# The passage from attention to the experts: where the last value sum, the selections, the token counts, the fourth weight split and the row scaling stand

## The chip, the cores and the metric

The kernel runs on one core of a Trainium2 chip. The core has five engines with a queue of instructions each: TensorE (PE, with its weight loads shown apart as PEld), VectorE (DVE), ScalarE (ACT), GpSimd (POOL) and SyncE (SP, which here only issues DMAs). Each engine starts its instructions in the order of its queue; an instruction that waits holds what is behind it. The metric is device microseconds (us) of one execution; the median of the runs shown counts.

## The reference

```python
q_bits = (einsum('bhsd,dk->bhsk', q, proj) > 0); k_bits = ...      # 6 bits: a bucket for each row
scores = where(q_bucket == k_bucket, q @ k.T / sqrt(64), -1e9)      # 2 x 8 heads, 768 rows, 64 wide
x = softmax(scores) @ v                                             # 1536 tokens x 512
e_idx = argmax(x @ w_gate)                                          # one expert of 8 for each token
out[mask_e] = gate_w * eom * (relu(x[mask_e] @ w1[e]) @ w2[e])      # 512 -> 1024 -> 512
y = elu(out @ w_in) @ w_out                                         # 512 -> 2048 -> 512
```

All of it is float32. The kernel splits each operand into a rounded high part and the remainder (hi and lo, `wh` and `wl`, `xh` and `xl`), and adds three products for one.

## The kernel before

There are three stages one after the other: attention (to about 257 us of the profiled span), the eight experts (267 to 443 us), and the wide layer (to the end). The order of the instructions on each engine is that of the program text, which is written by hand; nothing reorders it.

**End of attention.** `stage_V` (L405) multiplies the probabilities by the values for one half head `m` into a PSUM bank of the pool `ps_o`, which has one bank. `stage_O` (L424) copies it out to `osb` on ACT. The last `m` is `NM - 1`. `stage_R` (L471) turns `osb` into token rows. The pool `ps_s` (two double banks) held the scores, which are done by then.

**The last two groups of tokens.** Tokens come in four groups of 384 (`NG - 2` and `NG - 1` are the last ones), each of three columns `c` of 128. `gate` (L525) returns three lists for a group: `main` finds the expert and the row `rown`, and converts it to the index `idx` (the last two items, `main[15:]`); `after` counts the tokens of each expert into `cnt`; the third list, `scs` for the last group, scatters the 384 token rows to `xs_d` in HBM, with one indirect DMA by POOL for a column, at the place that `idx` names.

**The operand of expert 0.** It is not loaded from HBM. `part_sel` (L860) makes a matrix `sel` of zeros and ones that selects the tokens of a column, `part_head` (L864, ACT) and `part_rest` (L868, DVE) make the scaled rows `xhi` and `xlo`, and `part_move` (L874, PE) multiplies rows by `sel` into the accumulators `xacc`. In `first_xT` (L899) these products run in a fixed order, column by column; then ACT copies the two halves of `xacc` to `hi` (the tile `xt`), DVE takes the remainder `lo`, `totals` (L1045) multiplies `cnt` by ones on PE into `pso` and makes the tables `tab` and `offd` on DVE, and `keep_warm` (L621) issues products that nobody reads.

**Experts.** The weights of an expert come in eight pieces of 512 KB: four of `w1`, four of `w2`. `load_piece` (L98) loads a piece on SP, `split_piece` (L813) splits it (`wh` on ACT, `wl` on DVE) and then lets SP load more; a load waits until the split has freed one of the buffers `wraw`. The splits of pieces 1 to 3 stand ahead of expert 0 (`AHEAD = 4`; piece 0 is split earlier); piece 4 is split behind the second of the eight column blocks `f` of expert 0, piece 5 behind the fourth, piece 6 behind the sixth, piece 7 behind the eighth. `moe_L1` (L1111) takes twelve matmuls for a block into one of three banks `hps`, then ACT (`h`, L1124) and DVE (L1125) empty the bank. `moe_L2` (L1127) takes the eight blocks of `h` in turn into `yps`, four times for an expert. `load_xs` (L1090, SP) loads the rows of an expert from `xs_d`; for expert 1 it stands between the loads of pieces 5 and 6 and waits for the last scatter. `scale_xs` (L837) multiplies its two halves of 128 rows by the gate weight in place; `make_xT` (L1095) transposes them on PE, the first time behind the first `moe_L2` of the expert before.

Of the kernel before, what the change touches and what calls it, by code (L numbers as in the profile page):

```python
# [8 lines left out]
F32 = mybir.dt.float32  # L9
# [3 lines left out]
AF = mybir.ActivationFunctionType  # L13
# [12 lines left out]
def kernel(  # L26
# [15 lines left out]
    nc = tc.nc  # L42
    B, H, S, D = q.shape
    E, DM, F = w1.shape
# [5 lines left out]
    HC = HALF * 128  # L50
# [6 lines left out]
    CAP = 224  # L57
# [3 lines left out]
    NG = 2 * B  # L61
# [53 lines left out]
    ps_s = att.enter_context(tc.tile_pool(name="ps_s", bufs=2, space=PSUM))  # L115
    ps_t = att.enter_context(tc.tile_pool(name="ps_t", bufs=3, space=PSUM))
    ps_o = att.enter_context(tc.tile_pool(name="ps_o", bufs=1, space=PSUM))
# [285 lines left out]
    ops = {}  # L403

    def stage_V(m, part):  # L405
        hd = part_of(m)[0]
        hi, lo = ptt[m]
        if part == 0:
            ops[m] = ps_o.tile([128, HC], F32, tag="o", name="o")
        for kt in (2 * part, 2 * part + 1):  # L410
            for x, t in enumerate((hi, lo)):
                nc.tensor.matmul(  # L412
                    ops[m], vst[hd][:, kt, :], t[:, kt, :], start=(kt == 0 and x == 0), stop=(kt == NC - 1 and x == 1)
                )
# [201 lines left out]
    def both(fs):  # L616
        for f in fs:
            f()

    load_pair(1, "q")  # L620
    def keep_warm(n, end=False):  # L621
        ps = (ps_t if end else ps_o).tile([128, HC], F32, tag="t" if end else "o", name="warm")
        for i in range(n):
            nc.tensor.matmul(ps, ones_b, ones_b[:, None, :].to_broadcast([128, HALF, 128]), start=(i == 0), stop=(i == n - 1))
# [52 lines left out]
    NM = 2 * NH  # L677
# [101 lines left out]
    for pc in range(E * NP):  # L779
        stream.append((pc,))  # L780
        j, i = divmod(pc - W2P, 7)
# [23 lines left out]
    def narrow_ops(n):  # L805
        for _ in range(min(n, len(todo_w2))):
            todo_w2.pop(0)()
        load_ahead()

    AHEAD = 4  # L810
    wsp = {}

    def split_piece(pc, eng=nc.vector, eng_hi=nc.scalar, rest=None):  # L813
        if pc not in wraw:
            return
        r = wraw.pop(pc)
        p, a, n = (m2a, "v", 3) if 0 <= pc < 3 else (m1, "w", 5)
        hi = p.tile([128, PW], F32R, tag=a + "h", name="wh", bufs=n)
        lo = p.tile([128, PW], F32R, tag=a + "l", name="wl", bufs=n)
        if eng_hi is nc.scalar:  # L820
            eng_hi.activation(hi, r, AF.Copy)  # L821
        else:
            eng_hi.tensor_copy(hi, r)
        fs = [lambda: eng.tensor_tensor(lo, r, hi, ALU.subtract)]  # L824
        if rest is None:
            both(fs)
        else:
            rest.extend(fs)
        wsp[pc] = (hi, lo)
        assert stream[taken[0]] == (pc,)  # L830
        taken[0] += 1
        load_ahead()
# [4 lines left out]
    def scale_xs(e, engs):  # L837
        t = xsl[e]
        for a, eng in enumerate(engs):
            x, g = t[:, a, 0:DM], t[:, a, DM:DM + 1]  # L840
            if eng is None:
                continue
            if eng is nc.scalar:
                eng.activation(x, x, AF.Copy, scale=g)
            else:
                eng.tensor_scalar(x, x, g, None, ALU.mult)
# [13 lines left out]
    def part_sel(gi, c, eng=nc.vector):  # L860
        row0, sel = parts[gi][:2]
        eng.tensor_scalar(sel[:, c], ranks, row0[:, c:c + 1], None, ALU.is_equal)
# [5 lines left out]
    def part_rest(gi, c):  # L868
        _, _, xh, xl = parts[gi]
        xg = xw[divmod(gi, 2)]  # L870
        x, g = xg[:, c, 0:DM], xg[:, c, DM:DM + 1]
        nc.vector.scalar_tensor_tensor(xl[:, c], x, g, xh[:, c], ALU.mult, ALU.subtract)

    def part_move(gi, ps, which, dcs=range(KD), stop=None):  # L874
        sel = parts[gi][1]
        for c, i in which:
            y = parts[gi][2 + i]
            for dc in dcs:
                nc.tensor.matmul(
                    ps[dc], y[:, c, dc * 128:(dc + 1) * 128], sel[:, c],  # L880
                    start=((gi, c, i) == (NG - 2, 0, 0)), stop=((c, i) == stop),
                )
# [16 lines left out]
    def first_xT(acc, ps):  # L899
        xT[0] = [t.rearrange("p (c n) -> p c n", c=KD) for t in xt0]  # L900
        hi, lo = xT[0]
        part_move(NG - 2, ps, [(0, 1)])
        first_older(ps, 1)
        part_move(NG - 2, ps, [(1, 1)])
        part_move(NG - 1, ps, [(0, 0), (1, 0)])
        part_move(NG - 2, ps, [(2, 1)])
        part_move(NG - 1, ps, [(2, 0), (0, 1)])
        for i in range(2):
            part_move(NG - 1, ps, [(1, 1), (2, 1)], (2 * i, 2 * i + 1), (2, 1))
        for i in range(2):  # L910
            cs = slice(2 * i, 2 * i + 2)
            nc.scalar.activation(hi[:, cs], acc[i][:, :, 0:CAP], AF.Copy)
            nc.vector.tensor_tensor(lo[:, cs], acc[i][:, :, 0:CAP], hi[:, cs], ALU.subtract)
        totals()
        keep_warm(4, True)

    gates = {}

# [108 lines left out]
    first_older(old[1], 0)  # L1027
    keep_warm(3)
    part_rows(NG - 1)
    for c in (1, 2):  # L1030
        part_sel(NG - 1, c, nc.gpsimd)
    for c in range(HALF):
        part_head(NG - 1, c)
    part_rest(NG - 2, 1)
    part_sel(NG - 1, 0)
    both(main[15:])
    for gi, c in ((NG - 2, 2), (NG - 1, 0), (NG - 1, 1), (NG - 1, 2)):
        part_rest(gi, c)
    both(after)

    cno = gate_p.tile([128, 2, E], F32, name="cno")
    tab = gate_p.tile([1, 3 * E], I32, name="tab")
# [2 lines left out]
    def totals():  # L1045
        pso = ps_o.tile([128, 2, E], F32, tag="o", name="pso")
        nc.tensor.matmul(pso, ones_b, cnt[:, NG], start=True, stop=True)
        nc.vector.tensor_copy(cno, pso)
        nc.vector.tensor_copy(tab[:, 0:2 * E], cno[0:1].rearrange("p a e -> p (a e)"))
        nc.vector.tensor_reduce(tab[:, 2 * E:2 * E + 1], cno[0:1, 0], AX.X, ALU.max)  # L1050
        nc.vector.tensor_tensor(offd, cno[:, 1], ebase, ALU.subtract)
# [59 lines left out]
    def moe_L1(e, f, pc):  # L1111
        if f == 0:
            hT[e] = m1.tile([128, 2, FB1, CAP], F32R, tag="h", name="h")
        hi, lo = xT[e]
        wh, wl = (t.rearrange("p (c f) -> p c f", c=KD) for t in wsp[pc])
        fs = slice(f % 2 * 128, f % 2 * 128 + 128)
        ps = ps_h.tile([128, CAP], F32, tag="h", name="hps")
        terms = [(dc, w, x) for dc in range(KD) for w, x in ((wh, hi), (wh, lo), (wl, hi))]
        if (e, f) == (0, 0):
            terms = [(dc, w, x) for x in (hi, lo) for dc in range(KD) for w in ((wh, wl) if x is hi else (wh,))]  # L1120
        for i, (dc, w, x) in enumerate(terms):
            nc.tensor.matmul(ps, w[:, dc, fs], x[:, dc], start=(i == 0), stop=(i == len(terms) - 1))  # L1122
        h, l = hT[e][:, 0, f], hT[e][:, 1, f]
        nc.scalar.activation(h, ps, AF.Relu)  # L1124
        nc.vector.scalar_tensor_tensor(l, ps, 0.0, h, ALU.max, ALU.subtract)  # L1125
# [28 lines left out]
        nc.gpsimd.memset(x2h.bitcast(F32), 0.0)  # L1154
        nc.gpsimd.memset(x2l.bitcast(F32), 0.0)

    for i in range(1, AHEAD):
        split_piece(i)
        if i == 1:
            load_xs(1)  # L1160
    for e in range(E):
        if e == 0:
            off = 0
        else:
            off = nc.values_load(
                tab[0:1, E + e:E + e + 1], engines=[ENG.Activation, ENG.DVE], min_val=0, max_val=NT,
                skip_runtime_bounds_check_because="a count of some of the tokens",
            )
        for f in range(FB1):
            pc = e * NP + f // 2  # L1170
            moe_L1(e, f, pc)
            narrow_ops(1)
            if f == 1 and e + 1 < E:
                scale_xs(e + 1, (nc.gpsimd, nc.gpsimd))
            if f == 4 and e >= E - NG:
                tids(e - E + NG)
            if f % 2:
                wsp.pop(pc)
                split_piece(pc + AHEAD)
                if e == E - 1 and f == 7:  # L1180
                    split_w2(0)
                take_w2()
        if e == 0:
            first[0] = False
            load_ahead()
        for dc in range(KD):
            pc = e * NP + 4 + dc
            parts = moe_L2(e, dc, pc, off)
            if e == E - 1:
                parts()  # L1190
            narrow_ops(1)
            wsp.pop(pc)
            split_piece(pc + AHEAD)
            if e < E - 1:
                parts()
            if e + 1 < E and dc < 2:
                make_xT(e + 1, dc)
            if e == E - 1 and dc == 0:
                split_w2(1)
            take_w2()  # L1200
            if dc == 2 and e + 2 < E:
                load_xs(e + 2)
# [15 lines left out]
    acc = {}  # L1218
# [203 lines left out]
```

## Time and profile before

| | |
|---|---|
| median of 3 runs | 715.23 us (715.20 to 715.67) |
| profiled execution | 717.73 us, span of the trace 716.0 us |
| PE busy | 701.2 us (98% of the span), 4217 matmuls |
| DVE, ACT, POOL busy | 553.4 (77%), 428.8 (60%), 206.9 us (29%) |
| chain that ended last | PE 49%, issue 33%, DMA 7%, DVE 4%, ACT 3%, POOL 2% |
| mean granted TensorE clock | 0.998 of full speed |

PE is nearly always busy, so time is to be won or lost where PE waits. All that the change touches lies between 252 and 418 us. In the rows further down each line of a timeline is: start in us from the start of the span, duration in us, engine, line, operation, out<-in, shapes, count, and in brackets how long the engine had been idle before and what ended that.

### The profile page before, as it was taken

What the parts mean: (1) busy time and instruction counts of PE and PEld (TensorE: products, weight loads), DVE (VectorE), ACT (ScalarE), POOL (GpSimd) and SP (SyncE); (2) the same over time, 40 slices, a digit from 0 to 9 for tenths busy, and PEclk for the clock granted to TensorE, in tenths of its full rate; (3) what the DMA queues carried; (4) which work ended last, traced back from release to release, by engine and by line L of the source; (5) the groups of instructions that cost most, each with busy time, mean ns of one, the idle gap of its engine ahead of it and who ended that gap; (6) DMA issues with size and microseconds to landing.
All of it is one profiled execution on the core that took longest, in us unless ns stands there. A gap on an engine that the chain in (4) does not pass through costs nothing.

```text
span 716.0 us, 12241 instructions
## 1 busy us (share of the span) xinstructions
PE 701.2 (98%) x4217; PEld 627.7 (88%) x4218; DVE 553.4 (77%) x1043; ACT 428.8 (60%) x857; POOL 206.9 (29%) x507
## 2 busy tenths in 40 slices
PE   8999999999999999999999999999999999999996
PEld 6889999999998989999999989788888888888884
DVE  6979899899998887888888877977788546934433
ACT  5988898888888866666666665444443224422221
POOL 7655544555446471111144131000000000002012
PEclk9999999999999999999999999999999999999999
DMA  7856759577682319988788876222223000001011
GB/s 173 206 130 157 190 139 219 139 176 181 156 228 70 107 72 285 266 255 249 227 240 268 215 214 165 89 89 88 64 92 109 3 0 1 0 1 60 0 60 62
DMA packets 108565, 97.40 MB, mean 136 GB/s; under 512 B 33448, under 2 KB 94696, under 8 KB 108496
## 3 DMA queue, kind: packets, MB, share of 16 engines
q1 hardware_dynamic: 106032, 90.15, 46.8%
q0 software_dynamic: 2304, 6.40, 2.4%
q8 instruction: 35, 0.57, 0.3%
q14 instruction: 34, 0.28, 0.1%
q10 hardware_dynamic: 160, 0.00, 0.0%
HBM read 64.15 MB, written 10.72 MB: 105 GB/s over the span
## 4 chain that ended last, share of the span: by engine, by line
PE 49%; issue 33%; DMA 7%; DVE 4%; ACT 3%; POOL 2%; SPq 0%; POOLq 0%; ACTq 0%; DVEq 0%
PE hps L1122 10%; PE s L349 8%; PE o L412 7%; PE yps L1135 7%; PE t L396 7%; DMA out_dram<-part,tidt 5%; PE yps L1137 3%; PE sp L488 2%; ACT p L376 2%; PE zps L278 1%; PE prep L212 1%; DMA xs<-xs_d 1%; DVE nm L367 1%; PE xTp L1104 1%; DVE ptlo L399 1%
## 5 line engine op out<-in xcount | busy, mean ns | idle before, releaser
L399 DVE TENSOR_TENSOR ptlo<-t,pthi 128x384 fp32r<-128x384 f32 x192 | 99.9, 548 | 16.4 <-ACT pthi L398 14.7
L376 ACT ACTIVATE p<-s,bi,sc 128x768 f32<-128x768 f32 x96 | 96.1, 1001 | 19.7 <-POOL bi L369 18.0
L824 DVE TENSOR_TENSOR wl<-wraw,wh 128x1024 fp32r<-128x1024 f32 x63 | 77.1, 1226 | 22.2 <-ACT wh L821 20.6
L367 DVE TENSOR_REDUCE nm<-s 128x1 f32<-128x768 f32 x96 | 90.9, 947 | 0.3 <-PE s L349 0.3
L398 ACT ACTIVATE pthi<-t 128x384 fp32r<-128x384 f32 x192 | 84.7, 497 | 9.6 <-PE t L396 8.3
L1274 POOL DMA_INDIRECT out_dram<-part,tidt x12 | 11.5, 960 | 263.5 <-DVE part L1271 262.2
L1236 ACT ACTIVATE ee<-gps 128x512 f32<-128x512 f32 x48 | 28.7, 599 | 97.9 <-PE gps L1226 97.9
L1135 PE MATMUL yps<-h,wh 128*128 128x448 f32 x256 | 84.4, 380 | 0.0
L396 PE MATMUL t<-ident,p 128*128 128x128 f32 x576 | 79.6, 273 | 0.0
L1226 PE MATMUL gps<-x2h,vl 128*128 128x512 f32 x192 | 75.9, 395 | 0.0
L349 PE MATMUL s<-ka,qa 128*128 128x384 f32 x192 | 73.5, 384 | 2.2 <-ACT p L376 1.6
L1256 PE MATMUL a<-vh,gh 128*128 128x512 f32 x192 | 75.6, 394 | 0.0
L1256 PE MATMUL a<-vh,gl 128*128 128x512 f32 x192 | 75.4, 393 | 0.0
L1226 PE MATMUL gps<-x2h,vh 128*128 128x512 f32 x192 | 75.3, 392 | 0.0
L1226 PE MATMUL gps<-x2l,vh 128*128 128x512 f32 x192 | 75.2, 392 | 0.0
L1256 PE MATMUL a<-vl,gh 128*128 128x512 f32 x192 | 74.9, 390 | 0.0
L1239 ACT ACTIVATE gh<-ee 128x512 fp32r<-128x512 f32 x48 | 30.4, 633 | 69.2 <-DVE ee L1238 69.2
L1237 DVE TENSOR_SCALAR ee<-ee 128x512 f32<-128x512 f32 x48 | 20.4, 425 | 66.3 <-ACT ee L1236 66.2
L396 PEld LDWEIGHTS t<-ident,p 128*128 128x128 f32 x576 | 67.4, 140 | 4.1 <-DVE ptlo L399 0.5
L412 PE MATMUL o<-pthi,vst 128*128 128x384 f32 x192 | 67.1, 349 | 0.8 <-ACT osb L433 0.6
L821 ACT ACTIVATE wh<-wraw 128x1024 fp32r<-128x1024 f32 x63 | 66.1, 1052 | 0.9 <-DMA wraw<-in_moe_w_dram 0.9
L349 PE MATMUL s<-kb,qb 102*128 102x384 f32 x192 | 65.1, 340 | 0.2
(226 smaller groups left out, 1767.9 us busy)
## 6 DMA issues: line engine op xcount, KB each, us to landing
wraw<-in_moe_w_dram SPq DMA_DIRECT2D x64, 512.0 KB
w<-in_moe_w_in_dram SPq DMA_DIRECT2D x16, 512.0 KB
w<-in_moe_w_out_dram SPq DMA_DIRECT2D x16, 512.0 KB
ka<-khi SPq DMA_DIRECT2D x30, 192.0 KB
xs_d<-zt SPq DMA_DIRECT2D x8, 528.0 KB
xs<-xs_d SPq DMA_DIRECT2D x8, 528.0 KB
raw_k<-in_k_dram SPq DMA_DIRECT2D x16, 192.0 KB
raw_v<-in_v_dram SPq DMA_DIRECT2D x8, 384.0 KB
```

What stands on the lines that cost most here:

```text
L349: nc.tensor.matmul(ps[:, j, 0:HC], opnd[st, "q" + x][0:n1, cb], opnd[st, "k" + x][0:n1, j * HC:(j + 1) * HC], start=(x == "a"), stop=(x == ...
L367: nc.vector.tensor_reduce(nm, sps[n][:, :, 0:HC], AX.XY, ALU.max, negate=True)
L376: nc.scalar.activation(p.rearrange("p (a b) -> p a b", a=2), sps.pop(n)[:, :, 0:HC], AF.Exp, bias=bi, scale=sc, accum_out=sums[hd][:, c:c ...
L396: nc.tensor.transpose(ps[:, a, :], p[:, kt * 128:(kt + 1) * 128], ident)
L398: nc.scalar.activation(ho, ps, AF.Copy)
L399: nc.vector.tensor_tensor(lo[:, HALF * g:HALF * (g + 1), i * 128:(i + 1) * 128], ps, ho, ALU.subtract)
L412: nc.tensor.matmul(ops[m], vst[hd][:, kt, :], t[:, kt, :], start=(kt == 0 and x == 0), stop=(kt == NC - 1 and x == 1))
L824: fs = [lambda: eng.tensor_tensor(lo, r, hi, ALU.subtract)]
L1122: nc.tensor.matmul(ps, w[:, dc, fs], x[:, dc], start=(i == 0), stop=(i == len(terms) - 1))
L1135: nc.tensor.matmul(ps, wh[:, f], h[:, :, f], start=(f == 0), stop=last)
L1226: nc.tensor.matmul(ps, w[:, dc], x[:, dc, th * TC:(th + 1) * TC], start=(dc == 0 and i == 0), stop=(dc == KD - 1 and i == 2),)
L1256: nc.tensor.matmul(ps, x[:, cs], w, start=(fb in first_fb and i == 0), stop=(fb in last_fb and i == 2))
```

## The change

It has five parts.

1. The last value sum (`m == NM - 1`) goes to a bank of `ps_s` instead of the one bank of `ps_o`.
2. Of the last group's three selections two are made on DVE (columns 0 and 1, ahead of the `xlo` of the last two columns of group `NG - 2`) and one on POOL (column 2); before, POOL made columns 1 and 2.
3. In `first_xT` the second half of `hi` is copied by DVE instead of ACT; `main[15:]` (row and index) and `after` (the counts) stand behind the two `lo` on DVE, and `totals` behind them; two warming products instead of four, ahead of `totals`.
4. The split of piece 3 stands behind the first column block of expert 0.
5. For experts 1 to 7 POOL scales the first half of the rows only; ACT scales the second, behind the eighth column block of the expert before.

```diff
@@ stage_V
-            ops[m] = ps_o.tile([128, HC], F32, tag="o", name="o")
+            pool, tag = (ps_s, "s") if m == NM - 1 else (ps_o, "o")
+            ops[m] = pool.tile([128, HC], F32, tag=tag, name="o")
@@ first_xT
+        nc.scalar.activation(hi[:, 0:2], acc[0][:, :, 0:CAP], AF.Copy)
+        nc.vector.tensor_copy(hi[:, 2:4], acc[1][:, :, 0:CAP])
+        keep_warm(2, True)
         for i in range(2):
             cs = slice(2 * i, 2 * i + 2)
-            nc.scalar.activation(hi[:, cs], acc[i][:, :, 0:CAP], AF.Copy)
             nc.vector.tensor_tensor(lo[:, cs], acc[i][:, :, 0:CAP], hi[:, cs], ALU.subtract)
+        both(main[15:])
+        both(after)
         totals()
-        keep_warm(4, True)
@@ ahead of first_xT
     part_rows(NG - 1)
-    for c in (1, 2):
-        part_sel(NG - 1, c, nc.gpsimd)
+    part_sel(NG - 1, 2, nc.gpsimd)
     for c in range(HALF):
         part_head(NG - 1, c)
-    part_rest(NG - 2, 1)
-    part_sel(NG - 1, 0)
-    both(main[15:])
-    for gi, c in ((NG - 2, 2), (NG - 1, 0), (NG - 1, 1), (NG - 1, 2)):
+    for c in range(2):
+        part_sel(NG - 1, c)
+    for gi, c in ((NG - 2, 1), (NG - 2, 2), (NG - 1, 0), (NG - 1, 1), (NG - 1, 2)):
         part_rest(gi, c)
-    both(after)
@@ experts
-    for i in range(1, AHEAD):
+    for i in range(1, AHEAD - 1):
         split_piece(i)
         if i == 1:
             load_xs(1)
...
             moe_L1(e, f, pc)
+            if (e, f) == (0, 0):
+                split_piece(AHEAD - 1)
             narrow_ops(1)
             if f == 1 and e + 1 < E:
-                scale_xs(e + 1, (nc.gpsimd, nc.gpsimd))
+                scale_xs(e + 1, (nc.gpsimd, None))
+            if f == 7 and e + 1 < E:
+                scale_xs(e + 1, (None, nc.scalar))
```

How the order moves on PE, from the last products of `xacc` to the first of expert 0 (`pso` is the product of the counts, `warm` a warming product). Before, the rows from there on (three more pairs like the last follow, and then `hps`):

```order
L879 MATMUL xacc<-sel,xlo 128x224 x12
L1047 LDWEIGHTS ones_b
L1047 MATMUL pso<-cnt,ones_b 128x16
L624 LDWEIGHTS ones_b
L624 MATMUL warm<-ones_b 128x384
```

With the change:

```order
L880 MATMUL xacc<-sel,xlo 128x224 x12
L625 LDWEIGHTS ones_b
L625 MATMUL warm<-ones_b 128x384
L625 LDWEIGHTS ones_b
L625 MATMUL warm<-ones_b 128x384
L1048 LDWEIGHTS ones_b
L1048 MATMUL pso<-cnt,ones_b 128x16
L1123 MATMUL hps<-xt_4296,wh 128x224
```

The product of the counts, which was ahead of four warming products, is now the last instruction ahead of expert 0's first (`hps`), and it still reads `cnt`.

On DVE, from the row of the last group's first column (`row_4458`, what the selections compare with) to the remainder `xt`. Before:

```order
L852 SCALAR_TENSOR_TENSOR row_4458<-g_rk,ohs 128x3
L872 SCALAR_TENSOR_TENSOR xlo<-xw,xhi 128x512
L862 TENSOR_SCALAR sel<-ranks,row_4458 128x224
L587 TENSOR_REDUCE rown<-g_rk 128x3
L588 CAST g_idx<-rown 128x3
L872 SCALAR_TENSOR_TENSOR xlo<-xw,xhi 128x512
L872 SCALAR_TENSOR_TENSOR xlo<-xlast,xhi 128x512 x3
L561 TENSOR_REDUCE cnt<-ohs 128x8
L592 TENSOR_TENSOR g_lt<-g_fm,w_73 128x24
L565 TENSOR_REDUCE cnt<-g_lt 128x8
L569 TENSOR_TENSOR cnt<-cnt 128x16
L913 TENSOR_TENSOR xt_4297<-xacc,xt_4296 128x448 x2
```

With the change:

```order
L863 TENSOR_SCALAR sel<-ranks,row_4458 128x224 x2
L873 SCALAR_TENSOR_TENSOR xlo<-xw,xhi 128x512 x2
L873 SCALAR_TENSOR_TENSOR xlo<-xlast,xhi 128x512 x3
L912 CAST xt_4296<-xacc 128x448
L916 TENSOR_TENSOR xt_4297<-xacc,xt_4296 128x448 x2
L588 TENSOR_REDUCE rown<-g_rk 128x3
L589 CAST g_idx<-rown 128x3
L562 TENSOR_REDUCE cnt<-ohs 128x8
L593 TENSOR_TENSOR g_lt<-g_fm,w_73 128x24
L566 TENSOR_REDUCE cnt<-g_lt 128x8
L570 TENSOR_TENSOR cnt<-cnt 128x16
```

The index `g_idx` and the counts `cnt` moved from ahead of the remainder of `xacc` to behind it, and a second selection came in ahead of the first `xlo`. The order of SP's loads is the same before and after: piece 5, the rows of expert 1, piece 6, piece 7.

## Rows read from the trace of the kernel before

**Rows 1.** Who PE waited for, 266 to 446 us: us, times, longest.
```profile
PE xTp L1104 <- POOL xs L846: 1.4, 1, 1.4
PE hps L1122 <- DVE h L1125: 0.9, 1, 0.9
```

**Rows 2.** Timeline: the last value sum, and ACT between it and its copy.
```profile
253.42 0.44 PE L412 MATMUL o<-pthi,vst 128*128 128x384 f32 x1 [0.58 <-ACT osb L433]
...
255.38 0.71 ACT L844 ACTIVATE xs<-xs 128x512 f32<-128x512 f32 x1
...
256.00 0.47 ACT L433 ACTIVATE osb<-o 128x384 f32<-128x384 f32 x1
```

**Rows 3.** Timeline of DVE, 261 to 268 us.
```profile
261.69 0.52 DVE L862 TENSOR_SCALAR sel<-ranks,row 128x224 fp32r<-128x224 bf16 x1
262.14 0.16 DVE L587 TENSOR_REDUCE rown<-g_rk 128x3 f32<-128x24 f32 x1
...
262.41 0.74 DVE L872 SCALAR_TENSOR_TENSOR xlo<-xw,xhi 128x512 fp32r<-128x512 f32 x1
...
265.18 0.17 DVE L561 TENSOR_REDUCE cnt<-ohs 128x8 bf16<-128x24 bf16 x1
...
265.68 0.17 DVE L569 TENSOR_TENSOR cnt<-cnt 128x16 bf16<-128x16 bf16 x1
266.77 1.16 DVE L913 TENSOR_TENSOR xt<-xacc,xt 128x448 fp32r<-128x448 f32 x2 [0.92 <-ACT xt L912]
```

**Rows 4.** Timeline of PE, 264 to 272.6 us.
```profile
264.50 0.70 PE L879 MATMUL xacc<-sel,xhi 128*128 128x224 f32 x4 [0.57 <-POOL sel L862]
...
266.39 0.18 PE L1047 MATMUL pso<-cnt,ones_b 128*128 128x16 bf16 x1
...
266.94 0.40 PE L1122 MATMUL hps<-xt,wh 128*128 128x224 f32 x1
...
272.11 0.48 PE L1122 MATMUL hps<-xt,wh 128*128 128x224 f32 x2 [0.86 <-DVE h L1125]
```

**Rows 5.** Timeline of POOL: selections, first and last of three scatters, first scaling.
```profile
261.48 2.97 POOL L862 TENSOR_SCALAR sel<-ranks,row 128x224 fp32r<-128x224 bf16 x2
264.62 1.56 POOL L598 DMA_INDIRECT xs_d<-xlast,g_idx  x1 [0.17 <-issue]
...
267.76 0.96 POOL L598 DMA_INDIRECT xs_d<-xlast,g_idx  x1 [0.23 <-issue]
...
276.03 3.27 POOL L846 TENSOR_SCALAR xs<-xs 128x512 f32<-128x512 f32 x2 [7.23 <-DMA xs<-xs_d]
```

**Rows 6.** Timeline of SP's queue: rows of expert 1, then pieces 6 and 7.
```profile
270.64 0.37 SPq L1092 DMA_DIRECT2D xs<-xs_d  x1
271.13 1.45 SPq L107 DMA_DIRECT2D wraw<-in_moe_w_dram  x2
```

**Rows 7.** Timeline: split of piece 6, second layer's first and sixth block, blocks 7 and 8.
```profile
277.70 1.06 ACT L821 ACTIVATE wh<-wraw 128x1024 fp32r<-128x1024 f32 x1 [0.92 <-DMA wraw<-in_moe_w_dram]
...
278.90 0.38 PE L1135 MATMUL yps<-h,wh 128*128 128x448 f32 x1
...
279.94 0.68 DVE L1125 SCALAR_TENSOR_TENSOR h<-hps,h 128x224 fp32r<-128x224 f32 x2
...
280.49 0.38 PE L1135 MATMUL yps<-h,wh 128*128 128x448 f32 x1
```

**Rows 8.** Timeline around the first transposes for expert 7.
```profile
409.39 4.53 POOL L846 TENSOR_SCALAR xs<-xs 128x512 f32<-128x512 f32 x2 [15.22 <-DMA xs<-xs_d]
...
412.61 0.36 ACT L1140 ACTIVATE sum<-yps 128x224 f32<-128x224 f32 x1 [1.29 <-PE yps L1135]
...
413.98 0.55 PE L1104 MATMUL xTp<-ident,xs 128*128 128x128 f32 x3 [1.36 <-POOL xs L846]
```

**Rows 9.** The opening products; busy time, PEclk, DMA share, GB/s of a stretch.
```profile
1.16 4.98 PE L624 MATMUL warm<-ones_b 128*128 128x384 bf16 x15 [1.16 <-DVE eb_b L81]
...
268.00:272.00 4.00, 3.25 (x30) 3.06 (x28) 3.97 (x9) 3.65 (x7) 0.81 (x2) 1.00 0.65 227
```

## The prediction

> **What bounds it now.** I looked first at the shares: PE works nearly all the time, so only PE's waits matter. Then I read who PE waited for from the first expert to the wide layer. There are two waits in 180 us: 1.4 us for POOL's scaled rows and 0.9 us for DVE emptying a bank [rows 1]. Then I read the timelines of the passage, where PE waits for the copy of a value sum [rows 2] and for a POOL selection [rows 4]. Last I read what stands just behind each, because the change moves work onto DVE and ACT and past POOL's and SP's queues. All the waits that the change can remove come to 0.58 + 0.57 + 0.86 + 1.36 = 3.4 us, 0.5% of the run. A difference under 0.2%, or 1.43 us, is about what a measurement of this kernel cannot tell from none.
>
> **Part 1, the last value sum.** PE waited 0.58 us for the one bank [rows 2]. With a bank of its own the sum starts that much earlier. But its copy `osb` starts at 256.00, behind a row scaling on ACT that runs from 255.38 [rows 2] and depends on DVE, not on this sum. So the copy stays where it is, and only the products that do not read it move up: six of the twelve that follow then stand ahead of the copy's end, 256.47, and six behind it as before. I take 0.2 us; the bounds are 0 and 0.58.
>
> **Part 2, the selections.** PE waited 0.57 us for the last of two POOL selections, 1.5 us each [rows 4, 5]. One POOL selection then ends near 263.0 and its wait goes. But two selections on DVE now stand ahead of the `xlo` that the products need next; before, that `xlo` came first and one selection behind it. Selection to next operation is 0.45 us (261.69 to 262.14, [rows 3]), so that `xlo` comes 0.7 to 0.9 us later and PE, which took it at once, waits there instead. From there on 0.57 us of waiting is gone, and some tenths of smaller stops, so the last product of `xacc` comes when it came before. I take nothing; the bounds are 0.3 us either way.
>
> **Part 3, the counts.** Here a wait is added on PE. The count product stands directly ahead of expert 0's first product, and it needs `cnt`, which DVE now makes behind the remainder. DVE's chain, with 0.2 us taken off from part 1: the last product of `xacc` started just ahead of 266.39 [rows 4] and is there 0.2 us later, so DVE's copy of the second half starts at 266.6 - 0.2 = 266.4. It is not in the trace; the two remainders of that size take 0.58 us each [rows 3], and I take 0.5 us. The remainders end near 268.0. Then come row and index, 0.27 us (262.14 to 262.41), and the four counts, 0.67 us (265.18 to 265.85) [rows 3]. `cnt` is ready at 268.9, and the first `hps` starts at 269.0 instead of 266.94 [rows 4].
>
> That is 2.0 us later, but not 2.0 us lost. Before, PE stood 0.86 us ahead of the fourth block, at 272.11, because DVE had three weight splits ahead of the first bank to be emptied [rows 4]. **Part 4** puts the third split behind it. DVE then has two splits left, which it starts when `pso` is through; it empties the first bank near 272.3, and PE, 36 products of 0.118 us on (16 of that width took 264.50 to 266.39, [rows 4]), wants it at 273.2. So that wait goes, and the first layer is 2.06 - 0.86 = 1.2 us late (0.7 to 1.6 over the unknown copy and part 2).
>
> **What else the index holds up.** It also starts the scatters. The first started at 264.62 [rows 5] with POOL free after its selections; now it starts when `idx` is there, at 268.4: 3.8 us later. The load of expert 1's rows waits for the last scatter (it went out 2.9 us after that one started, [rows 5, 6]): it goes out at about 274.4 instead of 270.64. Piece 6 is queued behind it on SP and goes out at 274.9 instead of 271.13.
>
> Piece 6 had no room: ACT already waited 0.92 us for it, until 277.70 [rows 7]. ACT's copies of blocks 7 and 8 stand behind that split, and so do DVE's; block 7 was done at 280.28 (the first of two from 279.94 on), and the second layer, whose sixth block started 1.59 us after its first, at 280.49, wanted it at 280.8 [rows 7]. How fast does piece 6 land now? In 6.57 us, as before: 281.5. It came 7.06 us after the load of the rows, but then piece 5, issued little earlier, was in front (1.67 us lies between the landings of the rows and of piece 6, about the same size, [rows 5, 7]); without that, 279.8; and with each scatter as short as the last (0.96 for 1.56 us, [rows 5]) 279.2. I take the middle, 280.3. Block 7 is then done 2.58 us later, at 282.9, **2.0 us** behind 280.8. This contains the 1.2 us of part 3 and is not added to it: the later of the two counts. Bounds: 1.2 and 3.3 us.
>
> **Part 5, the scaling.** For expert 7 the rows landed at 409.39, POOL took 4.53 us for both halves, and PE stood 1.36 us [rows 8]. POOL's first half alone ends near 411.6. ACT stood idle for 1.29 us before 412.61, behind one split of 1.06 [rows 7, 8], so it is through with the last bank at 410.3 and takes 0.71 us for a half [rows 2]: both are there before PE asks, near 412.6. The wait goes: **-1.36 us** (0 if the rows land over a microsecond later). Seven scalings of 0.71 us come onto ACT; each is followed by a split and then by an idle wait for `yps`, 1.29 us in the case shown [rows 8], and so costs nothing. In the other experts POOL was in time anyway. Two warming products fewer lie inside PE's wait for the counts.
>
> **Sum.** +2.0 - 1.36 = +0.64 us: the profiled execution goes from 717.73 to about 718.4 us. That execution was 2.5 us above the median of the runs; by the median, 715.23 + 0.64 = **715.9 us**.
>
> **The clock, weighed against a rule.** PE will stand idle between the warming products (until 266.5) and 269.0, 2.5 us, longer than any stop in the experts so far. In the stretch with the 0.86 us stop the granted clock is 1.00, the 2.4 GHz level [rows 9]. No row shows a stop of 2.5 us, so I keep full speed. The Trainium skill, "TensorE: Matmul & The Clock Gate", section "Why this matters for your kernels", asks that PE not be left idle for long between bursts of matmuls, or it falls to the half clock; by it the sum could be as in rival B.
>
> **Rivals.**
> - **A, slower: piece 6 lands as late as it is issued.** If the DMA needs its 6.57 us again, expert 0 loses 3.3 us and the sum is +1.9: 717.2 us. It decides from a landing at 281.0 on. For it: the load of the rows took 5.4 us to land. Against: less is in flight.
> - **B, slower: PE falls to 1.2 GHz after the idle stretch.** The opening products, after no work, took 4.98 us [rows 9] for 15 of 384 columns: 0.86 ns a column, against 0.53 for the 224 columns in 0.118 us. If the first layer ran for 5 us at half speed, 2.5 us would be lost, of which the wait for block 7 hides about 1: +0.64 + 1.5 = +2.1, 717.4 us. Against: a stop of 2.5 us is not the start of a program.
> - **C, faster: neither new wait binds.** If the counts are ready sooner, because DVE's small operations overlap, and piece 6 lands by 278, what remains is -1.36 and some 0.3 us of parts 1 and 2: 713.6 us. Against: it needs both, and the order puts `cnt` and `idx` behind three operations of half a microsecond.
> - **D, slower: part 5 doesn't do it.** If the rows of expert 7 land after 410.4, ACT waits in place of POOL and PE still stands: +2.0, 717.2 us. Only expert 7's rows were that late.
>
> **How the numbers follow.** My forecast, 715.9 us with a range of its own of 715.1 to 716.6, has 0.53; A 0.20, B 0.06, C 0.14, D 0.07. Slower by over 0.2% is A, B and D: 0.33. Faster by over 0.2% is most of C: 0.12. Within is 0.55. The range from 713.5 to 717.6 takes in C at its price and leaves out its far half and the far ends of A and B, some 0.2 together.
>
> **What would show it.** The `hps` of expert 0 start near 269 with a wait for the counts ahead of them; no wait for `h` before the fourth block; scatters from 268.4; the load of expert 1's rows near 274.4; ACT waiting for piece 6 until about 280; PE standing some 1 us in the first `yps`; no wait for POOL at expert 7. I am wrong if PE starts `hps` before 268, if block 7 is done by 281, or if a stop stays at expert 7.

## The result, and the profile after

| | before | with the change |
|---|---|---|
| median | 715.3 us (715.20 to 715.67, 4 runs) | 722.0 us (720.12 to 722.58, 4 runs) |
| profiled execution | 717.73 us, span 716.0 | 722.58 us, span 720.9 |
| mean granted TensorE clock | 0.998 | 0.992 |

The ratio is 1.0087 [1.0074, 1.0100]: slower by 6.7 us, above the predicted range. The chain of events was the predicted one: late counts, late index, late scatters, late piece 6, a stop in the first `yps`. Two of its links were longer than I took them, the clock fell twice, and a gain was counted that wasn't there.

Who PE waited for with the change, 266 to 446 us (engine, tile and line waited for: us, times, longest), against [rows 1]:

```profile
PE pso L1048 <- DVE cnt L570: 2.3, 1, 2.3
PE yps L1136 <- DVE h L1126: 1.8, 1, 1.8
```

Both waits of before are gone, POOL's at expert 7 and DVE's ahead of the fourth block, and two larger ones stand in their place. The timeline of PE with the change, against [rows 4, 7]:

```profile
262.76 0.71 PE L880 MATMUL xacc<-sel,xlo 128*128 128x224 f32 x4 [1.10 <-DVE xlo L873]
...
269.25 0.18 PE L1048 MATMUL pso<-cnt,ones_b 128*128 128x16 bf16 x1 [2.31 <-DVE cnt L570]
269.28 0.35 PE L1123 MATMUL hps<-xt,wh 128*128 128x224 f32 x1
...
281.71 0.37 PE L1136 MATMUL yps<-h,wh 128*128 128x448 f32 x1
...
285.59 0.47 PE L1136 MATMUL yps<-h,wh 128*128 128x448 f32 x1 [1.83 <-DVE h L1126]
```

The counts made expert 0 start at 269.28, as forecast (269.0). The timeline of DVE, against [rows 3], shows why:

```profile
261.14 0.91 DVE L863 TENSOR_SCALAR sel<-ranks,row 128x224 fp32r<-128x224 bf16 x2
261.97 1.40 DVE L873 SCALAR_TENSOR_TENSOR xlo<-xw,xhi 128x512 fp32r<-128x512 f32 x2
...
266.63 0.62 DVE L912 CAST xt<-xacc 128x448 fp32r<-128x448 f32 x1 [1.27 <-PE xacc L880]
267.17 1.15 DVE L916 TENSOR_TENSOR xt<-xacc,xt 128x448 fp32r<-128x448 f32 x2
268.23 0.17 DVE L588 TENSOR_REDUCE rown<-g_rk 128x3 f32<-128x24 f32 x1
268.43 0.17 DVE L589 CAST g_idx<-rown 128x3 int32<-128x3 f32 x1
...
269.02 0.17 DVE L570 TENSOR_TENSOR cnt<-cnt 128x16 bf16<-128x16 bf16 x1
```

Copy, two remainders, index and counts stand one behind the other, from 266.63 to 269.19. Now the other branch, that of the index. POOL, against [rows 5] (first and last scatter, first scaling):

```profile
269.38 1.05 POOL L599 DMA_INDIRECT xs_d<-xlast,g_idx  x1 [7.06 <-ACT wh L822]
...
272.26 0.96 POOL L599 DMA_INDIRECT xs_d<-xlast,g_idx  x1 [0.21 <-issue]
...
280.74 1.58 POOL L847 TENSOR_SCALAR xs<-xs 128x512 f32<-128x512 f32 x1 [7.43 <-DMA xs<-xs_d]
```

SP's queue, against [rows 6] (piece 5, the rows of expert 1, piece 6 and what follows):

```profile
271.14 0.37 SPq L107 DMA_DIRECT2D wraw<-in_moe_w_dram  x1
276.75 0.37 SPq L1093 DMA_DIRECT2D xs<-xs_d  x1
277.23 14.93 SPq L107 DMA_DIRECT2D wraw<-in_moe_w_dram  x9
```

What SP's load of these rows waited for, 255 to 300 us, first before, then with the change:

```profile
SPq L1092 <- DMA xs_d<-xlast,g_idx: 0.6, 1, 0.6
SPq L1093 <- DMA xs_d<-xlast,g_idx: 5.1, 1, 5.1
```

ACT at piece 6, against [rows 7]:

```profile
282.92 1.06 ACT L822 ACTIVATE wh<-wraw 128x1024 fp32r<-128x1024 f32 x1 [3.33 <-DMA wraw<-in_moe_w_dram]
```

The load of the rows held SP's queue until 276.75 (forecast 274.4), piece 6 was split from 282.92 (forecast 280.3), and block 7 came for PE at 285.59. Last the stretches, with the busy time of each engine, the granted clock (the column behind POOL), DMA share and GB/s:

```profile
266.00:269.00 3.00, 0.93 (x8) 0.52 (x6) 2.29 (x8) 2.43 (x3) 0.00 (x0) 1.00 0.00 0
269.00:273.00 4.00, 3.75 (x20) 3.76 (x21) 3.30 (x8) 1.03 (x2) 3.19 (x5) 0.58 0.25 89
273.00:286.00 13.00, 11.17 (x94) 10.80 (x93) 7.19 (x11) 7.03 (x13) 1.88 (x3) 1.00 0.90 268
286.00:290.00 4.00, 4.00 (x19) 3.74 (x18) 3.59 (x5) 2.04 (x5) 0.00 (x0) 0.58 1.00 307
290.00:296.00 6.00, 6.00 (x40) 5.67 (x40) 3.41 (x6) 3.60 (x7) 0.00 (x0) 0.99 1.10 285
```

Behind each of the two stops the clock was at 0.58 on the mean of four microseconds: most of that time at the 1.2 GHz level, though PE was working in it. The whole execution shown has a mean granted clock of 0.992, as has one other of the four (722.09 us); the remaining two, which have no profile, show 0.996 (721.92 and 720.12 us), so the clock was low for less time in them.

**One table for all runs.** The start of the selection products wanders by 2 us between executions (255.3 to 257.5), so I count from the first `xacc` product to the first `hps` and first `yps` of expert 0, to the first `hps` of expert 1, and to the first product of the wide layer (`gps`), each read from the PE timeline of the profiled execution. The last column takes in seven more experts, so a few tenths there cannot be put down to one part. Each row is one execution, not always a usual one. Against its run's median, the profiled one was 2.5 us longer in the first row, about 1.3 in e1_warm and 1.2 in e3_index_warm, and 1.4 us shorter in p2_select and b1_best and 1.2 in a1_piece_first.

| run | hps | yps | expert 1 | gps | median us |
|---|---|---|---|---|---|
| before, profile shown | 9.73 | 21.69 | 32.71 | 186.28 | 715.3 |
| p0_before | 9.75 | 21.71 | 32.89 | 184.90 | 715.93 |
| the change | 12.19 | 24.62 | 39.28 | 191.29 | 722.0 |
| e1_warm | 12.21 | 23.01 | 39.41 | 191.44 | 721.82 |
| e2_index | 12.19 | 22.99 | 33.99 | 186.00 | 716.87 |
| e3_index_warm | 13.90 | 24.70 | 35.71 | 187.70 | 717.37 |
| e4_index_counts | 10.00 | 21.55 | 32.85 | 184.87 | 715.35 |
| p1_bank | 9.85 | 21.81 | 32.81 | 184.81 | 715.58 |
| p2_select | 9.82 | 21.78 | 32.79 | 184.80 | 716.4 |
| p4_split | 9.74 | 20.76 | 32.78 | 184.91 | 715.47 |
| p5_scale | 9.75 | 21.71 | 32.88 | 184.97 | 716.1 |
| a1_piece_first | 12.20 | 24.62 | 35.63 | 187.69 | 718.42 |
| a2_piece_first_warm | 12.20 | 23.00 | 36.46 | 188.64 | 720.32 |
| b1_best | 9.43 | 20.44 | 32.77 | 184.91 | 716.12 |
| b2_best_scale | 9.44 | 20.45 | 31.46 | 183.68 | 714.72 |

The change loses 2.44 us ahead of `hps`, 0.47 in the first layer, 3.48 in the second, and nothing from there to `gps`: 39.28 - 32.89 = 6.39 us against p0_before, which is the difference of the medians but for 0.3.

### The profile page after: what moved, and what is told of

Same layout as the page of the kernel before. It is cut to its first block, busy times and chain, and to the rows that moved or that the text cites. A ratio compares the mean times of both kernels' runs of the same rounds, so it can differ in the third digit from the quotient of the medians.

```text
span 720.9 us, 12247 instructions
## 1 busy us (share of the span) xinstructions
PE 703.7 (98%) x4215; PEld 630.4 (87%) x4216; DVE 554.1 (77%) x1045; ACT 432.4 (60%) x863; POOL 187.2 (26%) x499
## 4 chain that ended last, share of the span: by engine, by line
PE 51%; issue 33%; DMA 6%; DVE 4%; ACT 3%; POOL 2%; SPq 0%; POOLq 0%; ACTq 0%; DVEq 0%
PE hps L1123 11%; PE yps L1136 8%; PE s L349 8%; PE o L413 7%; PE t L396 7%; DMA out_dram<-part,tidt 5%; PE yps L1138 3%; PE sp L489 2%; ACT p L376 2%; PE zps L278 1%; PE prep L212 1%; DVE nm L367 1%; DVE ptlo L399 1%; PE xTp L1105 1%; DMA wraw<-in_moe_w_dram 1%
## 5 line engine op out<-in xcount | busy, mean ns | idle before, releaser
L1136 PE MATMUL yps<-h,wh 128*128 128x448 f32 x256 | 86.1, 385 | 1.8 <-DVE h L1126 1.8
```

Source lines behind the costliest of these rows:

```text
L1136: nc.tensor.matmul(ps, wh[:, f], h[:, :, f], start=(f == 0), stop=last)
```

## The experiments

"The change minus" a part starts from the changed kernel; "before plus" from the one before. Ratios are to the kernel before on the same chip.

**e1_warm: more warming products.**

```diff
-        keep_warm(2, True)
+        keep_warm(16, True)
```

> The change with 16 warming products instead of 2 ahead of the count product, so that TensorE works through its wait for the counts. Theory (the late scatters make piece 6 late, and that sets the end of expert 0): the granted clock stays at 1.00 from 266 to 274 us and the second layer is reached 1.7 us earlier, but piece 6 still lands near 282.9, block 7 is done when it was, TensorE stands about 3.5 us instead of 1.8 there and the clock still falls behind that stop. Time as with the change, 721.5 to 722.5 us. Rival 1 (the two falls of the clock are the loss): 1.7 to 3.4 us less, 718.6 to 720.3 us. Rival 2 (the wait for the counts is the loss): as with the change or 1.7 us less.

721.82 us, 1.0087 [1.0070, 1.0104]. Two of its stretches and its wait in the second layer:

```profile
269.00:273.00 4.00, 3.96 (x35) 3.54 (x33) 3.62 (x12) 1.31 (x2) 2.86 (x5) 1.00 0.24 89
...
286.00:290.00 4.00, 4.00 (x17) 3.76 (x18) 3.29 (x6) 3.15 (x5) 0.00 (x0) 0.62 0.98 317
```

```profile
PE yps L1136 <- DVE h L1126: 3.5, 1, 3.5
```

With PE busy until the counts came, the first fall of the clock is gone and `yps` starts 1.6 us earlier (23.01 for 24.62). The stop at piece 6 took all of it back: 3.5 us for 1.8. So piece 6 sets expert 0's end, and the second fall follows that stop.

**e2_index: the index early, the counts late.**

```diff
@@ first_xT
-        both(main[15:])
@@ behind the two selections on DVE
+    both(main[15:])
```

> The change with row and index of the last group back ahead of the remainders (behind the two selections on VectorE); the counts stay behind the operand split. Theory: the scatters start near 264.6, piece 6 lands before 279, no stop in the second layer of expert 0 and only the first fall of the clock is left: +2.3 (wait for the counts) - 0.9 + 1.7 (clock) - 1.4 (expert 7) = +1.7, about 717 us. Rival 1 (the falls of the clock alone): 1.7 us less than the change, 720.3 us. Rival 2 (the wait for the counts): as with the change, 722 us.

716.87 us (716.02 to 720.39), 1.0030 [1.0015, 1.0045]. The index's place is worth 5 us. What is left of the late counts is 33.99 - 32.89 = 1.10 us, the 1.2 us that the prediction gave to parts 3 and 4. In the profiled execution (716.03) the stops of 1.4 us at `xlo` and 2.0 us ahead of `pso` went by with the clock at full speed:

```profile
260.00:264.00 4.00, 2.61 (x24) 2.43 (x23) 3.97 (x9) 1.56 (x3) 2.98 (x6) 1.00 0.25 89
264.00:268.00 4.00, 1.97 (x18) 1.57 (x17) 2.52 (x8) 2.43 (x3) 1.65 (x4) 1.00 0.48 186
268.00:272.00 4.00, 4.00 (x37) 4.00 (x38) 3.83 (x8) 2.38 (x4) 0.00 (x0) 1.00 0.18 53
```

So the expected "about 717" came out by luck: it counted 1.7 us for a fall of the clock, which is not there, and took off 1.4 us for part 5, which gives nothing either (p5_scale). Seven of the ten executions (716.0 to 717.2 us) have a mean granted clock of 0.997 or 0.998; the other three (719.1 to 720.4 us) have 0.992 to 0.995, so in these the clock was low for longer.

**e3_index_warm: both of these.**

> Both of the two before: index early and 16 warming products. Theory: no fall of the clock, no stop at piece 6; the wait for the counts remains: +2.3 - 0.9 - 1.4 = 0, 715.0 to 715.8 us. The difference to the run with the index alone is what the clock costs by itself, 1.7 us. Rival 1: 718.6 us. Rival 2: 722 us or 1.7 us less.

A miss: 717.37 us, 1.0023 [1.0010, 1.0036], no faster than e2_index. The warming products were to win back a fall that most executions of e2_index do not have. The profiled execution, 718.57 us, shows another one. Two of its stretches:

```profile
262.00:264.00 2.00, 1.67 (x9) 1.67 (x9) 2.00 (x4) 0.17 (x1) 1.54 (x2) 0.64 0.00 0
264.00:266.00 2.00, 2.00 (x11) 2.00 (x11) 0.93 (x2) 0.00 (x0) 1.60 (x3) 0.50 0.53 200
```

The wait that precedes them:

```profile
262.33 1.00 PE L880 MATMUL xacc<-sel,xlo 128*128 128x224 f32 x4 [1.39 <-DVE xlo L873]
```

Here the clock fell earlier, behind the wait for `xlo` that part 2 makes, which no warming product covers. It cost 35.71 - 33.99 = 1.72 us against e2_index, whose wait there was as long and was not followed by a fall. So a stop of 1.4 us in that place is followed by a fall in one execution and not in another. Three of the ten executions, this one among them, have a mean granted clock of 0.995 (718.6 to 719.0 us); the other seven have 0.997 to 0.999 and a median of 716.73 us, against 716.53 us of the like seven of e2_index, which is the kernel before (715.46) and the 1.1 us of the late counts. The fall explains the three, not the miss.

**e4_index_counts: index and counts early, the rest of the change kept.**

```diff
@@ first_xT
-        both(main[15:])
-        both(after)
@@ behind the selections on DVE, and behind the last xlo
+    both(main[15:])
...
+    both(after)
```

> The change with index and counts both made where they were before (the counts ahead of the copies of xacc), so that the count product does not wait; the bank, the selections, the copy on VectorE, the later fourth split and the scaling on ScalarE stay. Theory: the first hps start near 266.8, no stop ahead of the fourth block, none at piece 6, none at expert 7: 715.3 - 0.9 - 1.4 - 0.2 = 712.6 to 713.2 us, faster than both kernels. Rival (one of the other parts costs something too): 714 us or more.

715.35 us, 1.0001 [0.9989, 1.0014]: the whole loss is gone, and the 2 to 3 us of gain that I still expected from the other parts is not there, a miss. The next runs take these singly.

**p0_before and p5_scale: the kernel before again, and with part 5 alone.**

```diff
-                scale_xs(e + 1, (nc.gpsimd, nc.gpsimd))
+                scale_xs(e + 1, (nc.gpsimd, None))
+            if f == 7 and e + 1 < E:
+                scale_xs(e + 1, (None, nc.scalar))
```

> The kernel before once more, nothing edited, for a second profile of it: the first had 717.73 us where the median is 715.3. Theory: the stops ahead of the fourth block of expert 0 (0.9 us) and at the transposes for expert 7 (1.4 us) are there again, and the first profile was long in the attention stage. Rival: the stop at expert 7 belongs to that one execution, and the profile is some 1.4 us shorter for lack of it; then part 5 had nothing to win.

> The kernel before with part 5 alone: GpSimd scales the first half of an expert's rows, ScalarE the second, behind the eighth block. Theory: the stop at expert 7 goes, 1.4 us less, 713.9 us. Rival (the stop is not there in most executions): 715.3 us. No fall of the clock in either.

715.93 us, 1.0005 [0.9996, 1.0014], and 716.10 us, 1.0008 [0.9999, 1.0017]. The only wait of PE from 266 to 446 us in p0_before:

```profile
PE hps L1122 <- DVE h L1125: 0.9, 1, 0.9
```

Its scaling for expert 7:

```profile
406.13 3.12 POOL L846 TENSOR_SCALAR xs<-xs 128x512 f32<-128x512 f32 x2 [12.86 <-DMA xs<-xs_d]
```

POOL took 3.12 us for what took 4.53 in [rows 8], on rows that were there 2.2 us earlier after the first `xacc` product, and PE's transposes followed without a wait. The profiles of p1_bank, p2_select and p4_split, which scale these rows as before, have no such wait either. The 1.36 us stop of the profile shown belonged to that one execution, which was 2.5 us above the median; it stands in the table as the 1.4 us by which that profile's last column exceeds p0_before's. Part 5 alone wins nothing.

**p4_split: before plus part 4.**

```diff
-    for i in range(1, AHEAD):
+    for i in range(1, AHEAD - 1):
...
+            if (e, f) == (0, 0):
+                split_piece(AHEAD - 1)
```

> The kernel before with part 4 alone: the split of piece 3 behind the first column block of expert 0. Theory: the stop ahead of the fourth block (0.86 us) goes, 714.4 us. Rival: the first layer is then held by the remainder of the operand or by a later bank, and the time stays at 715.3 us.

715.47 us, 0.9995 [0.9986, 1.0005], where 714.4 was expected. The stop ahead of the fourth block went (`yps` at 20.76 for 21.71), and a new one stands in the first `yps`:

```profile
PE yps L1135 <- DVE h L1125: 0.7, 1, 0.7
```

Even before the change piece 6 set expert 0's end; the stop ahead of the fourth block was hidden by it.

**p1_bank and p2_select: before plus part 1, before plus part 2.**

```diff
@@ p1_bank
+            pool, tag = (ps_s, "s") if m == NM - 1 else (ps_o, "o")
+            ops[m] = pool.tile([128, HC], F32, tag=tag, name="o")
@@ p2_select
-    for c in (1, 2):
-        part_sel(NG - 1, c, nc.gpsimd)
+    part_sel(NG - 1, 2, nc.gpsimd)
...
+    for c in range(2):
+        part_sel(NG - 1, c)
```

> The kernel before, with part 1 of the change alone: the last value sum in a bank of the scores' pool. Prediction's term: the 0.58 us stop ahead of the sum goes, 0.2 us is won (0 to 0.58), the rest is given back as a wait for the copy of the sum: 715.3 us. Rival: all of the stop is won, 714.9 us. Other rival: the copy on ScalarE stands where it stood, all is given back, 715.5 us.

> The kernel before with part 2 alone: two of the last three selections on VectorE ahead of the xlo, one on GpSimd. Theory: TensorE's stop at the GpSimd selection (0.57 us) goes and one of about 1 us comes ahead of the products of that xlo, so 715.3 to 715.8 us, with single executions 1 to 2 us longer where the granted clock falls behind the longer stop (one of the index kernels showed 0.75 to 0.82 from 260 to 268 us). Rival: the stop is only moved and costs nothing, 715.0 to 715.3 us and the clock stays at 1.00.

Part 1: 715.58 us, 0.9995 [0.9984, 1.0006]; the wait at the bank is replaced by one of 0.5 us for the copy. Part 2: 716.40 us (714.97 to 719.90), 1.0018 [1.0006, 1.0031]; DVE's wait takes the place of POOL's, and the way to `hps` stays (9.82 for 9.75):

```profile
PE xacc L879 <- DVE xlo L872: 1.1, 1, 1.1
```

Its profiled execution shows no loss, but at 714.97 us it is the fastest of the eleven; what the median lost is not in it. Nor can the two executions at 718.82 and 719.90 us be put down to a fall of the clock behind this wait: their mean granted clocks, 0.998 and 0.997, are those of the others (0.997 to 0.999). That cause stays open.

**a1_piece_first and a2_piece_first_warm: the change, with piece 6 loaded ahead of the rows.**

```diff
-        if i == 1:
+        if i == 2:
             load_xs(1)
@@ in a2_piece_first_warm only
-        keep_warm(2, True)
+        keep_warm(16, True)
```

> The change, with SP's load of piece 6 ahead of the load of expert 1's rows instead of behind it; nothing else. Index and counts stay late, so the scatters stay late too. Theory (the late index costs time through SP's queue: piece 6 stands behind a load that waits for the last scatter): piece 6 goes out when the split of piece 2 frees its buffer, near 272.3 us instead of 277.2, lands near 278.5, the 1.8 us stop in the first yps goes, and with it the second fall of the clock near 287 us. The wait for the counts and the first fall near 270 us stay. Time 722.0 - 1.8 - 1.7 = 718.5, between 717.8 and 719.0. Rival (the late scatters cost time through expert 1's own rows): the rows still land near 281 us, PE then waits for them at the first transposes of expert 1, and the time stays above 720.

> The change, with piece 6 loaded ahead of expert 1's rows and sixteen warming products instead of two ahead of the product of the counts. Theory: with the stop at piece 6 out of the way, the first fall of the clock is no longer hidden by that stop, so sixteen warming products now win its 1.7 us: granted clock 1.00 from 266 to 300 us, time 718.5 - 1.7 = 716.8, between 716.2 and 717.4. Rival (the clock has no part in it): the time equals that of the run with two warming products, within 0.5 us.

a1: 718.42 us, 1.0038 [1.0026, 1.0049], as expected. Index and scatters are as late as in the change; only SP's order differs:

```profile
269.33 1.50 SPq L107 DMA_DIRECT2D wraw<-in_moe_w_dram  x2
276.70 0.37 SPq L1093 DMA_DIRECT2D xs<-xs_d  x1
```

The stretches behind the counts and in the second layer:

```profile
268.00:271.00 3.00, 3.00 (x16) 3.00 (x16) 2.72 (x6) 0.67 (x2) 2.57 (x5) 0.50 0.45 122
...
284.00:290.00 6.00, 6.00 (x41) 5.66 (x41) 5.87 (x11) 5.25 (x10) 0.00 (x0) 1.00 1.12 329
```

The first fall stays, the stop at piece 6 and the second fall are gone: 39.28 - 35.63 = 3.65 us came from piece 6 standing in SP's queue behind a load that waits for scatters (3.6 us by the medians).

a2 is a miss: 720.32 us, 1.0060 [1.0042, 1.0078], slower than a1. Its clock stayed at 1.00 and `yps` came 1.6 us earlier, but then PE stood for the rows of expert 1:

```profile
PE xTp L1105 <- POOL xs L847: 1.4, 1, 1.4
...
PE yps L1136 <- DVE sum L1142: 0.6, 1, 0.6
```

So the late index costs in a second way, through the rows themselves. In a1 that was hidden because PE was slower: the first transposes stand 27.16 us behind the first `xacc` product there and 27.07 us here. A clock fall that delays PE costs nothing where PE would have had to wait anyway; that it was worth nothing in e1 and a2 doesn't mean that it is cheap. This explains why a2 is no faster than a1. That it is slower has to do with piece 7, for which ACT stood 2.59 us (1.46 in a1) and behind whose split DVE's `sum` came late. Counted from the first `xacc` product it was there 28.61 us on, for 27.32 in a1; why, no run tells.

**b1_best and b2_best_scale: before plus parts 1 and 4 and piece 6 ahead of the rows; then part 5 too.**

> The kernel before, with part 1 (bank), part 4 (split of piece 3 behind the first column block) and the load of piece 6 ahead of the load of expert 1's rows; selections, index, counts and scaling as before. Theory: the stop of 0.9 us ahead of the fourth block goes by part 4; the 0.7 us stop that took its place in the first yps goes because piece 6 is out near 269.5 us, not 270.1, and no longer waits for a scatter; part 1 gives 0 to 0.2. No stop over 0.3 us is left between 262 and 300 us, and the time is 715.5 - 0.9 - 0.1 = 714.5, between 714.2 and 714.9. Rival (piece 6 lands no earlier, since it was the DMA and not the queue that set its landing): the 0.7 us stop stays and the time is 715.3.

> The kernel of the run b1_best with part 5 added: the second half of the rows scaled on ScalarE behind the eighth column block. Theory: with piece 6 out of the way what is late next is the scaling of expert 1's rows on GpSimd, for which TensorE stood 1.11 us at its second transpose; ScalarE has that half done by then, so the stop goes, and expert 1's first product comes 31.7 us after the first product of the selections instead of 32.8. Time 716.1 - 1.1 = 715.0, between 714.4 and 715.4, under the 715.6 of the kernel before. Rival (the rows land too late for either engine): ScalarE waits in place of GpSimd, the stop stays within 0.3 us and the time is 716.1.

b1: 716.12 us, 1.0007 [0.9997, 1.0017], a miss: 714.5 was expected. Both stops at blocks went, and the next late item was the scaling of expert 1's rows:

```profile
PE xTp L1105 <- POOL xs L847: 1.1, 1, 1.1
```

b2: 714.72 us, 0.9987 [0.9978, 0.9996] (eleven executions of 713.69 to 715.63; a twelfth of 1781.91 has no profile and no explanation here). PE's waits in its profile from 250 to 310 us are these:

```profile
PE sp L489 <- ACT osb L434: 0.5, 1, 0.5
PE sp L553 <- DVE ohs L580: 0.2, 1, 0.2
PE xacc L880 <- DVE xlo L873: 0.2, 1, 0.2
```

Expert 0 has no stop left: expert 1 starts at 31.46 instead of 32.89. It is faster than both kernels, by 0.9 us than the one before. In b1 and b2 POOL's two selections also came in time (`hps` at 9.43 and 9.44 for 9.75): they took 2.20 us for 2.97 in [rows 5]; why, no run tells. How much of the gain the order of the loads makes, without parts 1, 4 and 5, was not run.

## Why the prediction was wrong

By its own steps, 715.9 predicted and 722.0 measured:

- **Part 1** (0.2 us won): nothing that can be measured in p1_bank; inside its bounds.
- **Part 2** (nothing, 0.3 either way): `xlo` is waited for instead of `sel`, and 9.82 for 9.75 us to `hps`. Right in the profile, though p2_select as a whole came out 1.3 us longer (ratio 1.0018) for a reason that stays open; that the new, longer stop can be followed by a fall of the clock (e3_index_warm) was not foreseen.
- **Part 3 with part 4** (`hps` at 269.0, the first layer 1.2 us late): 269.28, and 1.10 us in e2_index. Right. The copy by DVE took 0.62 us where I took 0.5.
- **The index** (2.0 us, bounds 1.2 and 3.3): here the main step failed. "The scatters from 268.4": 269.38, 0.78 us behind the index, which was ready at 268.60. The same 0.78 us lie there in e2, e4 and a1; the prediction had put this term at nothing. "The load of the rows at about 274.4": 276.75, since the last scatter was 4.5 us from its issue to that load, for 2.9 before. "Lands at 280.3": 282.92, near 5.7 us behind its issue. From the first `xacc` to block 7's product the way became 28.50 us (285.59 - 257.09) from 23.68 in p0_before (279.80 - 256.12): 4.8 us late instead of 2.0, beyond the upper bound of 3.3, which let piece 6 land slowly, but had the scatters start with the index and take no longer than before. Rival A's sign, a landing from 281.0 on, came, but not for its reason: piece 6 landed faster than A took it and was issued 2.3 us later than forecast.
- **The clock** ("I keep full speed"): wrong, rival B with a chance of 0.06 happened. Half speed followed the 2.31 us stop and again the 1.83 us stop, which no rival had. The first fall costs 1.6 us (24.62 for 23.01 in `yps`), but the stop at piece 6 hid it; the second was not hidden, and is taken to make up the rest, 39.28 - 32.89 - 4.8 = 1.6 us. Its stretch bears this out: four microseconds at 0.58 are 1.7 us of full speed lost. No run removed it alone. The Trainium skill, "TensorE: Matmul & The Clock Gate", section "Why this matters for your kernels", warns against idle gaps of PE between bursts of matmuls. The trace agrees that a gap can do it, with 0.58 behind each stop, but not on the length: the gaps that the section warns of are longer than the 2.31 and 1.83 us seen here.
- **Part 5** (-1.36 us): wrong; taken from one execution, whose stop p0_before does not have, and then added to the median of others. Rival D named the right outcome of this part with the wrong reason: nothing was late in the usual execution.

The sum with measured terms: 0.64 as predicted, + 1.36 (part 5 gives nothing), + 2.8 (piece 6), + 1.6 (second fall) = 6.4 us, against 6.7 measured. The last term is what the others leave of the table's 6.39, so the sum meets that by construction.

## What to carry to other kernels

Before moving a small operation, follow every DMA that starts from it, and then what stands behind that DMA's waiting load on the same queue: 0.3 us of index computation moved back by 6 us (262.33 to 268.43) cost 5 us, over 3.6 of them because a weight load stood behind a load that waits for scatters. Put a load that waits for late data behind the loads that wait for nothing; here that, with parts 1, 4 and 5, made the faster kernel, while each of these parts alone won nothing. A wait seen in one profiled execution is a term only if that execution lies at the median, or if a second profile shows it; the mean granted clock of each execution tells which of them a fall of the clock can explain.

## What was not expected of the hardware

**The clock fell behind stops of about two microseconds.** Half speed followed stops of 2.31 us (the change and a1), 1.83 and 3.53 us (the second layer), and 1.39 us in e3_index_warm; it did not follow 2.0 us in e2_index, nor 1.4 us there and in e4_index_counts. The length of the stop alone does not decide; what else does, these runs leave open. In the change the granted clock was 0.50 in every half microsecond from 270.0 to 273.0 and from 287.0 to 290.0 us.

**A scatter queues with the loads.** The DMA queues' packets, MB and share of the 16 engines in three one-microsecond stretches of the change, 273 to 276 us (`q0` carries POOL's scatters, `q1` SP's loads):

```profile
q1 hardware_dynamic: 420, 0.22, 72.3%
...
q1 hardware_dynamic: 451, 0.22, 74.9%
q0 software_dynamic: 39, 0.16, 40.5%
...
q0 software_dynamic: 116, 0.38, 95.2%
```

Piece 5, issued at 271.14 between the scatters, moved first, and most of the last two scatters behind it. In p0_before, 267 to 269 us, the scatters had the engines to themselves, because piece 5 was issued behind the last of them (268.43 and 266.68):

```profile
q0 software_dynamic: 73, 0.24, 61.5%
...
q0 software_dynamic: 77, 0.27, 69.1%
```

This is where the last scatter's 4.5 us instead of 2.9 came from as the packets show it. No run took piece 5 away to measure it alone, but a1 and a2 put piece 6 there too, and the time from the last scatter's issue to the load of the rows grew to 6.25 us (270.45 to 276.70) and 6.34 us (271.74 to 278.08).
